# The first MLP product in 64x64 array tiles instead of 64x128

## The chip, the cores and the metric

The kernel runs on one core of a Trainium2 chip. The metric is the device time of one execution in microseconds, with all loads from and stores to the chip's memory. All arithmetic is in fp32.

## The reference

An RWKV-7 recurrence over 768 time steps, for 4 batches of 8 heads of 40 columns, followed by an MLP with an exact GELU over the 3,072 x 320 matrix that the heads make up:

```
for t in range(S):                       # S = 768, D = 40
    y[:, :, t] = einsum('bhd,bhde->bhe', rt, state)
    Sa = einsum('bhde,bhe->bhd', state, at)
    state = state * wt[:, :, None, :] - einsum('bhd,bhe->bhde', Sa, bt) \
            + einsum('bhd,bhe->bhde', vt, kt)
x = y.transpose(0, 2, 1, 3).reshape(B * S, H * D)     # 3072 x 320
h = x @ w_in                                          # 320 x 2048
g = 0.5 * h * (1 + erf(h / sqrt(2)))
out = g @ w_out                                       # 2048 x 320
```

## The kernel before

The 768 time steps are cut into 12 chunks of 64 (`c` is the chunk). In a chunk the recurrence is written as products: decays and their cumulative sums, the matrices `N` and `A`, the inverse of a triangular matrix (POOL builds it block by block, line 961 and line 963), the update of the state `st`, and `y`. Nearly all of these products are small: 64 or 40 rows by 64 columns of the TensorE array, with 64 or 104 columns streaming, or 32 by 32. They are issued through `mm` (line 193) in fours, so that each of the four 64x64 quarters of the array has one. In the timeline they are the groups of L193 with `64*64`, `40*64` or `32*32` (rows and columns of the array in use).

The result of a chunk, transposed, lies in `xt`: 5 slices of 64 of the 320 inputs, each with 256 columns (64 time steps of 4 batches). Both halves of the 128 partitions hold the inputs.

The MLP of a chunk is worked off between the attention steps of the following chunk. The step `mh(c, p)`, p from 0 to 7, is the first product. `w_in_sb` holds one half of the 2,048 hidden columns in each half of the partitions; a step takes 128 columns of each half, and for each of the 5 slices (`kt`) issues one matmul for each half `x`. Such a matmul uses 64 rows and all 128 columns of the array and streams 256 columns; the two halves' matmuls run at the same time, one in the upper and one in the lower 64 rows. The results accumulate over `kt` in PSUM, in one bank for each x; two steps (s = 0 and 1) fill the two halves of both banks. Then `ge(c, q)` applies GELU on ACT (line 1312) into `gt`, and frees the banks. The second product (line 1346, and line 1428 in the first chunks) uses 128 rows by 128 columns of the array. It is done by Strassen's scheme in seven products, with sums on DVE.

The order of all steps is written out by hand in `order(...)`, one list of tokens in which each token is one step. It sets the order of instructions on every engine at once: each step's instructions go to the engines' queues in the order of the list, and no engine changes it. The steps named in this text are in it as, for example, `mh.3.6 mh.3.7 ... ge.3.3`. PSUM is four pairs of banks, given out by `take` and given back by `drop`, in the same order.

Of the kernel before, what the change touches and what calls it, by code (L numbers as in the profile page):

```python
# [118 lines left out]
def kernel(  # L119
# [12 lines left out]
    nc = tc.nc  # L132
    B, H, S, D = r.shape
    DM, DF = moe_w_in.shape
    P = 128
    C = 64
    HP = 64
# [6 lines left out]
    NK = -(-DM // HP)  # L144
# [17 lines left out]
    def tile_of(name, shape, dtype=FP32):  # L162
        return const.tile(shape, dtype, name=name)
# [25 lines left out]
    def half(j, n=HP):  # L189
        return slice(j * HP, j * HP + n)  # L190
# [13 lines left out]
    xt = tile_of("xt", [P, NK, TB])  # L204
# [11 lines left out]
    w_in_sb = tile_of("w_in_sb", [P, NK, DF // 2])  # L216
# [1084 lines left out]
    @step  # L1301
    def mh(c, p):
        q, s = p // 2, p % 2
        ph = (bank if s else take)(f"ph{c}_{q}").rearrange("p x (s t) -> p x s t", s=2)
        for kt in range(NK):
            for x in range(2):
                nc.tensor.matmul(ph[:, x, s], w_in_sb[half(x), kt, p * P:(p + 1) * P], xt[half(x), kt],  # L1307
                                 start=kt == 0, stop=kt == NK - 1)

    @step  # L1310
    def ge(c, q):
# [155 lines left out]
```

## Time and profile before

| | us |
|---|---|
| three timed runs, median | 640.84 |
| lowest and highest | 638.62 and 642.05 |
| span of the profiled execution | 638.6 |
| TensorE busy in it | 621.4 |
| mean granted clock of TensorE | 0.995 of full |

The page gives no time for the profiled execution other than its span, from its first to its last instruction. In the rows below, an instruction group is written as line, engine, operation, written tile `<-` read tiles, then for TensorE rows`*`columns of the array in use, then partitions x elements of the operand, its type, and the count. PE is the matmul itself, PEld the load of the stationary operand. The profile shows each fp32 matmul as two records, and its weight load as two also. In a timeline row the first number is the start, the second the length from the first start to the last modelled end, in us; since matmuls overlap, a row can begin before the one ahead of it has ended.

### The profile page before, as it was taken

To read this page: it belongs to the slowest core of one execution; us is meant where nothing else is said; L and a number is where in the kernel's file an instruction comes from. 1 tells how busy PE (TensorE), PEld (TensorE's weight loads), DVE (VectorE), ACT (ScalarE), POOL (GpSimd) and SP (SyncE) were. 2 spreads that over 40 slices of the span, in tenths; PEclk is the share of its full clock that TensorE was granted. 3 is DMA by queue.
4 is the path that set the end of the run, shared out by engine and by line. 5 is a ranking of instruction groups with operands and counts; after the bars stand their busy time and mean duration, and the time that the engine had idled before them with its cause. 6 is when DMAs were issued, how large, how long until landed. Compare 5 with 4: busy or idle time off the path is not lost.

```text
span 638.6 us, 27896 instructions
## 1 busy us (share of the span) xinstructions
PE 621.4 (97%) x12418; PEld 548.3 (86%) x12418; DVE 457.9 (72%) x557; ACT 323.6 (51%) x456; POOL 380.3 (60%) x782
## 2 busy tenths in 40 slices
PE   7798999989999999999999999999999999999997
PEld 4576887778988988998998998998988998989987
DVE  0889889869887987875978877984883974753313
ACT  4468797874463465635544536563563365052021
POOL 4388289806845866848968548968805867910000
PEclk9799999999999999999999999999999999999999
DMA  9999488747478248395647445449346214210100
GB/s 136 181 162 178 91 178 187 143 104 137 91 135 149 59 98 159 64 147 111 110 84 133 76 93 107 88 88 157 68 92 109 41 37 84 42 26 3 36 7 21
DMA packets 246899, 64.07 MB, mean 100 GB/s; under 512 B 228380, under 2 KB 243644, under 8 KB 246780
## 3 DMA queue, kind: packets, MB, share of 16 engines
q1 hardware_dynamic: 246340, 62.01, 52.5%
q8 instruction: 97, 1.59, 1.1%
q10 hardware_dynamic: 440, 0.29, 0.2%
q14 instruction: 22, 0.18, 0.1%
HBM read 54.39 MB, written 3.93 MB: 91 GB/s over the span
## 4 chain that ended last, share of the span: by engine, by line
PE 76%; ACT 2%; DVE 0%; issue 0%; DVEq 0%
PE bank L1307 30%; PE bank L1346 27%; PE bank L193 19%; ACT Tt L937 0%; ACT SM L1154 0%; ACT L1312 0%; ACT spare L922 0%; DVE spare L864 0%; ACT st L1194 0%; ACT gt L1312 0%; ACT T L942 0%; DVE Tt L932 0%; ACT st L1192 0%; ACT Tt L1116 0%; DVE os L1299 0%
## 5 line engine op out<-in xcount | busy, mean ns | idle before, releaser
L1307 PE MATMUL bank<-xt,w_in_sb 64*128 64x256 f32 x1920 | 221.3, 381 | 0.2 <-ACT gt L1312 0.2
L961 POOL TENSOR_TENSOR tmp<-W,Nb 128x126 f32<-128x126 f32 (+22 forms) x341 | 164.4, 482 | 93.1 <-DVE Nb L927 67.6
L1307 PEld LDWEIGHTS bank<-xt,w_in_sb 64*128 64x128 f32 x1920 | 182.5, 187 | 25.1 <-issue 1.5
L963 POOL TENSOR_TENSOR W<-W,tmp 128x126 f32<-128x126 f32 (+22 forms) x341 | 168.8, 495 | 26.7
L1346 PE MATMUL bank<-w_out_sb,gt 128*128 128x160 f32 x704 | 101.1, 301 | 0.0
L1346 PEld LDWEIGHTS bank<-w_out_sb,gt 128*128 128x128 f32 x704 | 96.6, 190 | 2.2 <-issue 1.2
L1312 ACT ACTIVATE gt<-bank 128x1024 f32<-128x1024 f32 x48 | 48.7, 1024 | 94.9 <-PE bank L1307 94.6
L1175 DVE TENSOR_TENSOR SM<-bank,upper 128x832 f32<-128x832 f32 (+1 forms) x24 | 23.0, 988 | 20.3 <-PE bank L193 20.2
L1263 ACT COPY conv<-st 32x128 f32<-32x128 f32 (+2 forms) x55 | 28.0, 509 | 17.0 <-DVE st L1257 16.2
L1299 DVE TENSOR_TENSOR conv<-gt 128x1024 f32<-128x1024 f32 x11 | 14.2, 1290 | 25.1 <-ACT gt L1312 25.0
L1227 DVE TENSOR_TENSOR st<-bank,st 128x832 f32<-128x832 f32 (+1 forms) x22 | 21.2, 985 | 14.0 <-PE bank L193 14.0
L1346 PE MATMUL bank<-extra,conv 128*128 128x160 f32 x208 | 30.3, 300 | 0.0
L1299 DVE TENSOR_TENSOR os<-os,bank 128x160 f32<-128x160 f32 x44 | 13.8, 315 | 22.1 <-PE bank L1346 20.5
L1346 PEld LDWEIGHTS bank<-extra,conv 128*128 128x128 f32 x208 | 28.9, 190 | 0.1
L721 DVE TENSOR_TENSOR_SCAN kT<-spare,kT 128x256 f32<-128x256 f32 x36 | 26.6, 798 | 0.6 <-ACT kT L714 0.6
L1346 PE MATMUL bank<-extra,gt 128*128 128x160 f32 x176 | 25.8, 300 | 0.0
L1346 PEld LDWEIGHTS bank<-extra,gt 128*128 128x128 f32 x176 | 24.5, 190 | 0.1
L789 POOL TENSOR_TENSOR bk_rows<-bk_rows,part 128x640 f32<-128x640 f32 x9 | 14.3, 1591 | 14.3 <-ACT part L742 13.9
L1312 ACT ACT_TABLE_LOAD x17 | 21.8, 1283 | 0.3
L1346 PE MATMUL bank<-extra,SM 128*128 128x160 f32 x144 | 21.2, 300 | 0.0
L193 PEld LDWEIGHTS bank<-SM,Tt 64*64 64x64 f32 x768 | 17.1, 133 | 4.2 <-issue 2.3
L193 PE MATMUL bank<-SM,Tt 64*64 64x104 f32 (+1 forms) x768 | 19.3, 249 | 0.9 <-ACT Tt L1113 0.9
(220 smaller groups left out, 1101.1 us busy)
## 6 DMA issues: line engine op xcount, KB each, us to landing
bk_rows<-in_b_dram SPq DMA_DIRECT2D x24, 160.0 KB
bk_rows<-in_k_dram SPq DMA_DIRECT2D x24, 160.0 KB
out_dram<-os SPq DMA_DIRECT2D x46, 80.0 KB
VR<-in_v_dram SPq DMA_DIRECT2D x22, 160.0 KB
w_tile<-in_w_dram SPq DMA_DIRECT2D x36, 80.0 KB
a_pairs<-in_a_dram SPq DMA_DIRECT2D x18, 144.0 KB
a_pairs<-in_b_dram SPq DMA_DIRECT2D x18, 144.0 KB
v_pairs<-in_w_dram SPq DMA_DIRECT2D x18, 144.0 KB
```

The lines of the kernel that those rows point to most:

```text
L193: nc.tensor.matmul(o, lhsT, rhs, start=first, stop=True, skip_group_check=True)
L721: nc.vector.tensor_tensor_scan(logs[:, at:at + n], onward, logs[:, at:at + n], 0.0, ALU.mult, ALU.add)
L789: (nc.vector if q == "v" else nc.gpsimd).tensor_tensor(to, rows(k_of(c)), decays(c), ALU.mult)
L961: nc.gpsimd.tensor_tensor(t, W[:, BL // 2 - rows:, rest:rest + 1].to_broadcast([P, rows, rest]), Nb[:, rest:rest + 1, :rest].to_broadcast( ...
L963: nc.gpsimd.tensor_tensor(own, own, t, ALU.add)
L1175: nc.vector.tensor_tensor(SM[:, g, :, :, cols], pair_of(f"S{c}_", g).rearrange("p x i c -> p i x c")[:, :, :, cols], kept, ALU.mult)
L1227: nc.vector.tensor_tensor(to, pair_of(f"QY{c}_", g)[:, :, :, cols], to, ALU.add)
L1263: nc.scalar.copy(apart.rearrange("p e i g d -> p (e i g) d")[to_rows, :, to_col:to_col + n], st.rearrange("p e i g c -> p (e i g) c")[rows ...
L1299: nc.vector.tensor_tensor(to, one_, other, how)
L1307: nc.tensor.matmul(ph[:, x, s], w_in_sb[half(x), kt, p * P:(p + 1) * P], xt[half(x), kt], start=kt == 0, stop=kt == NK - 1)
L1312: nc.scalar.activation(gt[:, 4 * q:4 * q + 4].rearrange("p (x s) t -> p x s t", x=2), bank(f"ph{c}_{q}").rearrange("p x (s t) -> p x s t", ...
L1346: nc.tensor.matmul(po[:, n, :DM // 2], l_[:, f], r_[:, f], start=f == 0, stop=f == NF // 2 - 1)
```

## The change

In the step `mh` every matmul of 64 rows by 128 columns is split into two of 64 rows by 64 columns, one for each half of the 128 hidden columns. The four matmuls of one `kt` (two halves x of the rows, two halves of the columns) go to the four quarters of the array, in the order (upper rows, left columns), (lower, right), (upper, right), (lower, left). Each streams the same 256 columns as before, and each result lands where it did before: partitions 0 to 63 or 64 to 127 of the bank of x. A step has 20 matmuls instead of 10. The list in `order` and all other steps are unchanged.

```
         for kt in range(NK):
-            for x in range(2):
-                nc.tensor.matmul(ph[:, x, s], w_in_sb[half(x), kt, p * P:(p + 1) * P], xt[half(x), kt],
-                                 start=kt == 0, stop=kt == NK - 1)
+            for y in range(2):
+                for x in range(2):
+                    at = p * P + (x ^ y) * HP
+                    nc.tensor.matmul(ph[half(x ^ y), x, s], w_in_sb[half(x), kt, at:at + HP], xt[half(x), kt],
+                                     start=kt == 0, stop=kt == NK - 1, skip_group_check=True)
```

Here `P` is 128, `HP` is 64, `half(j)` the 64 partitions from 64 j on, and `ph` the pair of PSUM banks.

## The prediction

> **What bounds the kernel now.** I read the page first, then the timeline of TensorE alone, then its waits and the busy time by stage.
>
> ```profile
> span 638.6 us, 27896 instructions
> PE 621.4 (97%) x12418; PEld 548.3 (86%) x12418; DVE 457.9 (72%) x557; ACT 323.6 (51%) x456; POOL 380.3 (60%) x782
> PE 76%; ACT 2%; DVE 0%; issue 0%; DVEq 0%
> L1307 PE MATMUL bank<-xt,w_in_sb 64*128 64x256 f32 x1920 | 221.3, 381 | 0.2 <-ACT gt L1312 0.2
> ```
> ```profile
> 76.40:139.00 62.60, 59.61 (x1260) 48.05 (x1250) 52.53 (x73) 52.78 (x74) 44.53 (x77) 1.00 0.70 149
> 139.00:602.00 463.00, 462.25 (x9313) 420.59 (x9312) 343.55 (x387) 217.86 (x313) 293.77 (x590) 1.00 0.50 92
> ```
>
> TensorE is the bound: 97% busy, 76% of the chain that ended last. The stage table (length, then busy us of PE, PEld, DVE, ACT, POOL, then the granted clock) says it more sharply: from 139 to 602 us TensorE is idle for 0.75 us of 463, at the full granted clock. In that stage the next engine, DVE, has 343.55 us of work, 74%. The changed line, L1307, fills 221.3 us of the span, a third. So two questions decide: does TensorE need more or less time for L1307 and for what borders on it, and can the other engines follow.
>
> Busy time can't answer the first, because matmuls overlap. I read starts instead. The timeline of TensorE (start, length, then the group with its count):
>
> ```profile
> 291.07 4.59 PE L1307 MATMUL bank<-xt,w_in_sb 64*128 64x256 f32 x40
> 295.59 1.66 PE L193 MATMUL bank<-SM,Tt 64*64 64x104 f32 x64
> 297.18 2.43 PE L1307 MATMUL bank<-xt,w_in_sb 64*128 64x256 f32 x20
> 299.53 1.66 PE L193 MATMUL bank<-VR,bk_rows 64*64 64x104 f32 x64
> 301.01 1.61 PE L193 MATMUL bank<-SM,bk_rows 64*64 64x104 f32 x64
> 302.44 0.72 PE L193 MATMUL bank<-w_tile,cum_m 64*64 64x320 f32 x8
> 303.09 4.59 PE L1307 MATMUL bank<-xt,w_in_sb 64*128 64x256 f32 x40
> ```
>
> One step `mh` is 20 records: ten matmuls, and the profile shows each fp32 matmul as two records. Two tiles run at once, so 20 records are 10 waves of two. The bursts of 40 and of 20 differ by 4.59 - 2.43 = 2.16 us for 10 waves: **0.216 us a wave**, or 0.84 ns for each of its 256 columns. The whole step's streaming is 96 steps x 10 waves x 0.216 = 207 us of the 221.3.
>
> The rest is at the borders of the bursts. A burst of 20 begins at 297.18 and what follows begins at 299.53: 2.35 us, where 10 waves are 2.16, so 0.19 over. The burst of 40: 295.59 - 291.07 = 4.52, where 20 waves are 4.32: 0.20 over. I take 0.20 a burst. Half of it is the first wave:
>
> ```profile
> L1307 PE MATMUL bank<-xt,w_in_sb x1920: 376/376/480, 76.6 to 619.2; 64*128 64x256 f32 x192
> L1307 PEld LDWEIGHTS bank<-xt,w_in_sb x1920: 182/187/187, 76.6 to 619.0; 64*128 64x128 f32 x192
> L193 PEld LDWEIGHTS bank<-SM,Tt 64*64 64x64 f32 x768 | 17.1, 133 | 4.2 <-issue 2.3 <-POOL W L963 1.4 <-ACT conv L612 0.4
> ```
>
> The slowest matmul of L1307 takes 480 ns, the median 376: 0.10 us in which weights are loaded that in later waves load behind a running wave. The other 0.10 is paid on leaving.
>
> The attention bursts of 64 records (16 waves of four) show the same borders from their side. From 301.01 to 302.44, with 64-by-64 work before and after, is 1.43 us, or 0.0894 a wave. The one from 299.53 to 301.01, which comes out of L1307 and is followed by 64-by-64 work, takes 1.48: coming out of L1307 costs it 0.05. The one from 295.59 to 297.18 lies between two bursts of L1307 and takes 1.59: going into L1307 costs a further 0.11. So a border between 64x128 and 64x64 tiles is dear on both sides, and one between two kinds of 64x64 work costs nothing that these rows show. That it is the tile shape in the array and not the rows in use is seen here, where 64-row and 40-row work meet:
>
> ```profile
> 324.30 1.66 PE L193 MATMUL bank<-VR,late 64*64 64x104 f32 x64
> 325.78 1.11 PE L193 MATMUL bank<-rT,turned 40*64 40x64 f32 x64
> 326.82 4.59 PE L1307 MATMUL bank<-xt,w_in_sb 64*128 64x256 f32 x40
> ```
>
> 324.30 to 325.78 is 1.48 again: dear on entry from a 128-by-128 product, free on the way out to 40x64 work.
>
> **The change, part by part.** *The waves.* Each 64x128 matmul becomes two of 64x64, so a wave has four records in place of two, 960 waves as before, each still streaming 256 columns. The question is whether four tiles stream as fast as two. The four-tile rows say yes: 0.0894 us for 104 columns is 0.86 ns a column. The single-tile product is at 0.90:
>
> ```profile
> L1346 PE MATMUL bank<-w_out_sb,gt 128*128 128x160 f32 x704 | 101.1, 301 | 0.0
> 302.71 0.45 PE L193 MATMUL bank<-w_tile,cum_m 64*64 64x320 f32 x4
> ```
>
> That is 101.1 / 704 = 0.144 us for 160 columns. The longest four-tile wave, the second one of the 302.44 burst, starts at 302.71, so 0.27 us for 320 columns, 0.84 ns. Streaming does not depend on how many tiles share the array; this term is 0. Its bounds come from the same rows: at 0.86 ns a column a wave is 0.220 us, 960 x 0.004 = 4 us slower; at 0.83 (0.2125 a wave, rounding of the starts) 3 us faster. I take 0, from the row nearest in length, 320 columns.
>
> *Weight loads.* Two of 128 columns (187 ns) become four of 64 (133 ns). Inside a burst they hide behind the wave: in the 64x64 bursts four of them fit behind 0.0894 us, here they have 0.216. Without that cover a load would cost what it does at a first wave. Only the first wave after a border shows it: there 0.10 for 128 columns, 0.05 for 64.
>
> *The borders.* The timeline holds 48 bursts of L1307. Before 31 of them stands 64-column tile work, before 14 32-by-32 work, before 3 128-by-128 or other full-array work. After 36 stands 64-by-64 work, after 10 32-by-32, after 2 the second product. First and last of the 31 entries and of the 36 exits:
>
> ```profile
> 75.78 0.86 PE L193 MATMUL bank<-aT,nT 40*64 40x64 f32 x45
> 76.58 7.27 PE L1307 MATMUL bank<-xt,w_in_sb 64*128 64x256 f32 x60
> 83.77 0.41 PE L193 MATMUL bank<-VR,late 64*64 64x104 f32 x8
> ...
> 581.30 1.05 PE L193 MATMUL bank<-SM,Tt 64*64 64x64 f32 x60
> 582.29 2.43 PE L1307 MATMUL bank<-xt,w_in_sb 64*128 64x256 f32 x20
> 584.65 0.56 PE L193 MATMUL bank<-VR,bk_rows 64*64 64x64 f32 x22
> ```
>
> After the change L1307 has the same tile shape as that work, so those borders should go: an entry saves 0.11 + 0.10 = 0.21, an exit 0.10 + 0.05 = 0.15. The other 17 entries keep their border and save only 0.05 of first load; the other 12 exits save nothing. Sum: 31 x 0.21 + 36 x 0.15 + 17 x 0.05 = 6.5 + 5.4 + 0.85 = **12.8 us**.
>
> *What is late next.* The order on every engine is kept, and no DMA, wait or queue entry moves; each step after a burst simply starts earlier on TensorE. Whether its operands are there is seen in TensorE's waits; those from 76 to 139 us, then one row of those after:
>
> ```profile
> PE bank L193 <- ACT Js L1091: 1.5, 1, 1.5
> PE bank L193 <- ACT gt L1312: 1.4, 1, 1.4
> ...
> PE bank L1307 <- ACT gt L1312: 0.2, 1, 0.2
> ```
> ```profile
> 138.25 0.22 PE L193 MATMUL bank<-Tt,Js 32*32 32x32 f32 x2 [1.52 <-ACT Js L1091]
> ```
>
> The first ends at 138.25 us. At such a place TensorE already waits for another engine, and what it gains before is waited away, unless that engine too is served earlier. Four bursts lie before it, at three times about 0.36 and once 0.20: 1.3 us that I count as lost. After 139 us the view has no wait for another engine of over 0.2 us, and DVE at 74% has room, so I count the rest as kept: 12.8 - 1.3 = **11.5 us**.
>
> The profiled execution's span is 638.6; the timed runs go from 638.62 to 642.05 with the median 640.84, 2.2 above the span. I expect a span of about 627.1 and a median of 640.84 - 11.5 = **629.3**.
>
> *A rule of the skill that speaks against the change.* Against the 0.0894 us in which a wave of four records passes stands the Trainium skill, "TensorEngine Tiling (Array Packing)", Instruction Overhead: each matmul carries some 60 cycles of overhead on trn2. Were that charged for each of the 1,920 added records one after another, it would be an estimate from that page of 1,920 x 25 ns (60 cycles at the 2.4 GHz that the skill's page "TensorE: Matmul & The Clock Gate" gives) = 48 us, and the time would be about 677. This trace disagrees so far: at 25 ns a record four of them would need 0.100 us, more than the 0.0894 measured.
>
> **The rivals.** *Slower, two column tiles of one row half get in each other's way.* In the changed step tiles (row half x, columns 0 to 63) and (row half x, columns 64 to 127) stream the same 256 columns of `xt`, some ns apart. In the four-tile bursts above, the two tiles of a row half stream different columns; so no row shows this exact pattern. If they took turns, a wave would take 0.43 in place of 0.216: 960 x 0.216 = 207 us more, 836 in all. It decides from 0.012 us a wave (11.5 / 960), a wave of 0.228. Against it: four streams at once cost nothing in two row kinds.
>
> *Slower, the added records are not hidden.* The price from rows: 0.0894 / 4 = 0.0224 us a record, as an upper bound. 1,920 x 0.0224 = 43 us, so 629.3 + 43 = 672. It decides from 6 ns a record (11.5 / 1,920). Against it: a wave of four needs at most 0.0894 us for all its records and has 0.216. This is the mechanism of the skill's rule above.
>
> *Faster, but by about half.* The steps after a burst are attention steps that hang on DVE and ACT copies. If the 36 exits give their 0.15 back as new waits, 5.4 us go: 11.5 - 5.4 = 6.1, so 634.7. For it: 2.9 us of waits before 139 us show that such places exist. Against it: there is almost no wait later.
>
> *No change.* The border stays, because what is dear is not the tile shape but, say, the change of weights or of PSUM bank: then only the first loads shrink, 48 x 0.05 = 2.4 us, 638.4. Against it: the free borders at 301.01, 302.44 and 325.78, where weights and banks change too.
>
> **How the numbers follow.** About 0.5%, 3.2 us, is what a measurement of this kernel can tell from no change; the three runs spread over 3.4. Forecast, with its loss anywhere between nothing and a third: 0.66. Half of it: 0.16. No change: 0.08. Column tiles in each other's way: 0.06. Records not hidden: 0.04. So faster 0.82, same 0.08, slower 0.10. The low end: 12.8 kept in full plus the 3 us bound of the waves is 625.0; I stop at 625.5. The high end takes in the half case with the waves' upper bound partly paid: 636.5. What lies outside, the no-change case and the slower ones, has 0.18.
>
> **What would show it.** L1307 should be 64*64 64x256 with 3,840 records at a mean near 376 ns and weight loads at 133. A lone burst of one step between 64-by-64 work should last 2.16 us from its start to the next start, not 2.35, and a 64-record burst between two of them 1.43, not 1.59. TensorE's busy time should fall by about the time saved. A wave over 0.228 us, or new TensorE waits on ACT or DVE of over 0.15 us after most bursts, would make the prediction wrong.

## The result and the profile after

| | before | after |
|---|---|---|
| timed runs, median | 641.34 us of 4 | 649.3 us of 4 |
| lowest and highest | 638.62 and 642.05 | 645.87 and 650.47 |
| span of the profiled execution | 638.6 | 646.9 |

The ratio is 1.0123, with a 95% interval of 1.0087 to 1.0159: slower by 8 us, where 11.5 us of gain were forecast. The profiled execution after has a time of its own, 648.82 us, so 1.9 us lie around its span.

From the page of the kernel after (span, busy time, the DMA queue that carries instructions, the chain, the groups of the changed line):

```profile
span 646.9 us, 31736 instructions
PE 617.4 (95%) x14338; PEld 530.9 (82%) x14338; DVE 457.3 (71%) x557; ACT 323.9 (50%) x456; POOL 379.6 (59%) x782
q8 instruction: 112, 1.84, 1.3%
PE 74%; issue 2%; ACT 2%; DVE 1%; DVEq 0%; ACTq 0%
L1309 PE MATMUL bank<-xt,w_in_sb 64*64 64x256 f32 x3840 | 224.5, 379 | 6.7 <-issue 6.0
L1309 PEld LDWEIGHTS bank<-xt,w_in_sb 64*64 64x64 f32 x3840 | 161.3, 133 | 52.0 <-issue 11.1
```

The changed line runs as meant: 3,840 records of 64*64, mean 379 ns, loads of 133 ns. TensorE is busy for less time than before, 617.4 us against 621.4, and the span is still longer. So its idle time has grown: 638.6 - 621.4 = 17.2 us before, 646.9 - 617.4 = 29.5 us now, 12.3 more. In the chain the item issue has gone from 0 to 2%; it means that TensorE waited for nothing that the profile shows. The stage table (columns as in the prediction's) and TensorE's waits of the kernel after:

```profile
76.40:139.00 62.60, 60.14 (x1444) 46.76 (x1437) 53.20 (x74) 53.82 (x74) 44.93 (x77) 0.99 0.69 145
139.00:602.00 463.00, 449.95 (x10852) 399.75 (x10853) 341.80 (x385) 217.29 (x312) 292.52 (x590) 1.00 0.49 92
```
```profile
PE bank L193 <- issue: 10.1, 9, 2.2
PE bank L1309 <- issue: 6.0, 8, 1.2
PE bank L193 <- ACT Js L1091: 1.5, 1, 1.5
```

From 139 to 602 us TensorE now idles for 13.05 us, where it idled for 0.75. And the idle time has one name: issue, 16.1 us in 17 waits. Before there were three such waits and 2.5 us, a row of the waits of before that the prediction did not use:

```profile
PE bank L193 <- issue: 2.5, 3, 1.9
```

The timeline of TensorE after, the stretch that the prediction read in the kernel before:

```profile
283.99 2.77 PE L1309 MATMUL bank<-xt,w_in_sb 64*64 64x256 f32 x45
287.96 4.53 PE L1309 MATMUL bank<-xt,w_in_sb 64*64 64x256 f32 x75 [1.20 <-issue]
292.43 0.75 PE L193 MATMUL bank<-turned,spare 32*32 32x32 f32 x64
293.11 1.16 PE L193 MATMUL bank<-aT,kT 40*64 40x64 f32 x64
...
296.50 0.21 PE L193 MATMUL bank<-T,Js 32*32 32x32 f32 x2 [1.65 <-issue]
...
296.75 4.55 PE L1309 MATMUL bank<-xt,w_in_sb 64*64 64x256 f32 x80
301.11 1.61 PE L193 MATMUL bank<-SM,Tt 64*64 64x104 f32 x64
302.54 2.34 PE L1309 MATMUL bank<-xt,w_in_sb 64*64 64x256 f32 x40
304.70 1.61 PE L193 MATMUL bank<-VR,bk_rows 64*64 64x104 f32 x64
306.12 1.61 PE L193 MATMUL bank<-SM,bk_rows 64*64 64x104 f32 x64
```

Two things stand here. The forecast's borders are gone, to the digit: the lone step from 302.54 to 304.70 takes 2.16 us (2.35 before), the 64-record burst from 301.11 to 302.54 takes 1.43 (1.59 before). And two waits have come, one in the middle of a burst of the changed step, one in the middle of a group of 32-by-32 products, whose operands were all there. The saving at the borders is the forecast's too: from 301.11 to 306.12 are 5.01 us, where the same three bursts took 5.42 (295.59 to 301.01). That is 0.41 us, and the forecast was 0.21 for an entry, 0.15 for an exit and 0.05 for the exit of the burst ahead. Following the same matmuls through both traces, the places where the kernel after gains 0.1 us or more sum to some 12 us, and the places where it loses to some 19. Both sums shift by several us with which neighbouring shifts are taken as one place; only their difference is firm.

**Where the waits stand.** The queue that carries instructions has 112 packets in the page of after (above); the page of before has

```profile
q8 instruction: 97, 1.59, 1.1%
```

Both give 16.4 KB a packet. The change adds 1,920 matmul records and 1,920 records of weight loads to TensorE's stream, 3,840 instructions for 15 packets: **256 a packet**. And TensorE's 2 x 14,338 instructions of after make up 112 such blocks. A block is thus 128 matmul records with their loads. Counted in order, the waits of over 0.3 us in the kernel after begin at records 348, 985, 2257, 3148, 4295, 5443, 5698, 6463, 6719, 7994, 8632, 9015, 9907, 10291, 11184 and 12461. Their remainders by 128 fall evenly from 92 to 45, with no exception, because the stream also holds 116 instructions that wait for semaphores: counted with these, every wait stands at remainder 193 or 194 by 256. So each wait stands on the border of a block. In the rows above, 75 + 64 + 64 records and 53 of the 32-by-32 group lie between the two waits: 256 records, two blocks.

The packet records of the trace give the rest. For two waits of the kernel after (us: first record of the block, packet of the next block starts and lands, first record of the next block):

```
block begins   packet starts   packet lands   next block begins
   282.78         284.98          286.41           287.96
   292.89         293.95          295.15           296.50
```

My theory (A) from here: a block is fetched while the one ahead of it runs, and the fetch takes some 3.5 us or more from border to border. A block used up sooner leaves TensorE waiting for the rest. The second row's block held 1.97 us of work, and 1.97 + 1.65 of waiting is 3.62. The rivals: the four tiles disturb each other, or each added record costs time by itself, wherever it stands.

The firm part of A is the packet's landing. In all the kernels of this document, no block begins less than 1.19 us after its packet has landed, and every block that begins after a wait of over 0.3 us begins 1.20 to 1.87 us after it. The 3.6 us are only a rule of thumb, since packets do not start at a fixed time after a border. The first row's block held 3.98 us of work, more than 3.6, but the packet of the next one started only 2.20 us into it, and TensorE waited 1.20 us. Others start up to 3 us before the block ahead of theirs has begun to run. What sets their start was not tried.

### The profile page after: what moved, and what is told of

It is laid out like the page before. It is cut to its first block, busy times and chain, and to the rows that moved or that the text cites. A ratio compares the mean times of both kernels' runs of the same rounds, so it can differ in the third digit from the quotient of the medians.

```text
span 646.9 us, 31736 instructions
## 1 busy us (share of the span) xinstructions
PE 617.4 (95%) x14338; PEld 530.9 (82%) x14338; DVE 457.3 (71%) x557; ACT 323.9 (50%) x456; POOL 379.6 (59%) x782
## 4 chain that ended last, share of the span: by engine, by line
PE 74%; issue 2%; ACT 2%; DVE 1%; DVEq 0%; ACTq 0%
PE bank L1309 29%; PE bank L1348 26%; PE bank L193 18%; DVE kT L721 0%; ACT L1314 0%; ACT L734 0%; ACT spare L922 0%; ACT T L942 0%; ACT Tt L937 0%; DVE spare L864 0%; ACT wpT L734 0%; ACT st L1194 0%; ACT kT L738 0%; ACT gt L1314 0%; DVE Tt L932 0%
## 5 line engine op out<-in xcount | busy, mean ns | idle before, releaser
L1309 PE MATMUL bank<-xt,w_in_sb 64*64 64x256 f32 x3840 | 224.5, 379 | 6.7 <-issue 6.0
L1309 PEld LDWEIGHTS bank<-xt,w_in_sb 64*64 64x64 f32 x3840 | 161.3, 133 | 52.0 <-issue 11.1
L1299 DVE TENSOR_TENSOR conv<-gt 128x1024 f32<-128x1024 f32 x11 | 14.1, 1280 | 24.3 <-ACT gt L1314 24.2
L1299 DVE TENSOR_TENSOR os<-os,bank 128x160 f32<-128x160 f32 x44 | 13.8, 314 | 21.8 <-PE bank L1348 20.1
L193 PE MATMUL bank<-SM,Tt 64*64 64x104 f32 (+1 forms) x768 | 20.6, 248 | 1.8 <-issue 1.5
L193 PEld LDWEIGHTS bank<-SM,Tt 64*64 64x64 f32 x768 | 19.0, 133 | 3.7 <-issue 2.3
```

The source lines that it names most:

```text
L193: nc.tensor.matmul(o, lhsT, rhs, start=first, stop=True, skip_group_check=True)
L1299: nc.vector.tensor_tensor(to, one_, other, how)
L1309: nc.tensor.matmul(ph[half(x ^ y), x, s], w_in_sb[half(x), kt, at:at + HP], xt[half(x), kt], start=kt == 0, stop=kt == NK - 1, skip_group_ ...
```

## The experiments

**The old tiles with the new number of records.** Each matmul keeps its 64x128 tile and is split into two of 128 streaming columns.

```
-            for x in range(2):
-                nc.tensor.matmul(ph[:, x, s], w_in_sb[half(x), kt, p * P:(p + 1) * P], xt[half(x), kt], ...)
+            for u in range(2):
+                for x in range(2):
+                    nc.tensor.matmul(ph[:, x, s, u * P:(u + 1) * P], w_in_sb[half(x), kt, p * P:(p + 1) * P],
+                                     xt[half(x), kt, u * P:(u + 1) * P], ...)
```

> The step mh keeps its 64x128 tiles, two at once, but each matmul is split in two of 128 streaming columns, so it has 40 matmul records and 40 weight loads as in the changed kernel. Theory A (instruction supply: TensorE's instructions arrive in blocks of 256 and a block that is used up in less than about 3.5 us makes the engine wait for the next): no border is saved, the waits on issue appear as in the changed kernel, 10 to 22 us more than before, 651 to 663 us. Theory B (the four 64x64 tiles disturb each other, or the tile shape itself makes the waits): the tile shape is the old one, so only 960 x 2.3 ns = 2 us for the doubled number of waves, 643 us, and no new waits on issue.

Measured: 660.85 us against 640.12, ratio 1.0324 (1.0266 to 1.0381), within the range of A. Its waits:

```profile
PE bank L193 <- issue: 8.8, 8, 2.3
PE bank L1308 <- issue: 3.3, 7, 0.9
```

The waits come without any new tile, so disturbed tiles can't be their cause; a price for each added record they don't yet exclude. This kernel is 20.7 us above its runs of before, the kernel after 8.0 above its own. The difference, 12.8 us (20.73 - 7.96), is close to what the prediction had worked out for the borders, but it is not their price. From its start to the next group's, a burst of two steps takes 4.665 us here and one of one step 2.432, so a step's streaming takes 2.233 us where it took 2.16: some 7 us over the 96 steps. The expectation had put the doubled waves at 2 us. The waits on issue are 4.1 us fewer than in the kernel after (12.1 against 16.1), and three stretches of 3.4 us after 139 us are at half clock, where the kernel after has one, from 137.3 us.

**The new tiles with the old number of records.** The loop over y runs once, so half of the first product is left out, and a wave has two 64x64 records.

```
-            for y in range(2):
+            for y in range(1):
```

> The step mh uses 64x64 tiles but only two of the four (upper rows with left columns, lower rows with right columns), so half of the first product is left out; records stay at 20 per step and each wave still streams 256 columns. Theory A: the borders go and no waits on issue come, 641.3 - 12.8 = 628.5 us, 625 to 631. Theory B with the tile shape as the cause: the waits on issue stay, 640 us or more. (B with four tiles as the cause agrees with A here.)

Measured: 632.63 us against 640.12, ratio 0.9875 (0.9835 to 0.9916). That is 1.6 us above the range of A. In the trace the gains sum to some 12 to 13 us, again by which shifts are taken together. Two issue waits are left: 1.93 us at the start, where before has 1.92, and 0.64 us at one later border. Other waits take back some 5 us; the largest:

```profile
PE bank L751 <- DMA r_pairs<-in_r_dram: 1.5, 1, 1.5
```

So the tile shape saves about what was forecast, and 7.5 us of it reach the end when no block is added.

**The kernel before, moved by half a block.** 32 tiny products (32x32) are added in the warm-up step, four instructions each: 128 instructions. All the rest is as before, but the block borders fall elsewhere in it.

```
+        for n in range(32):
+            mm(pt[:BL, 0, :BL], w_in_sb[:BL, 0, :BL], w_in_sb[:BL, 0, :BL])
```

> The kernel before, with 32 tiny 32x32 matmuls (64 matmul records and 64 weight loads, 128 instructions) added at the start, at about 25 us where TensorE waits for loads. Theory A: the same work, but each border of an instruction block falls 128 instructions earlier in the work; the order before has its borders where a block lasts long, and half a block on they fall in the attention bursts: 5 to 15 us slower, 646 to 656, with waits on issue. Theory B and any theory of engines or tiles: under 1 us, 641 to 642.

Measured: 664.89 us against 640.12, ratio 1.038 (1.0332 to 1.0429). That is 24.8 us more, and 9 us above the range of A. The products themselves, run at half clock at the start, take 2.0 of it (the warm-up takes 4.79 us in before and 6.80 here). Waits, then the timeline where the prediction's first rows lay:

```profile
PE bank L193 <- issue: 14.1, 11, 2.1
```
```profile
296.28 0.75 PE L193 MATMUL bank<-turned,spare 32*32 32x32 f32 x64
296.96 1.16 PE L193 MATMUL bank<-aT,kT 40*64 40x64 f32 x64
...
300.00 0.21 PE L193 MATMUL bank<-Tt,Js 32*32 32x32 f32 x2 [1.32 <-issue]
```

The short attention products now fill one block by themselves: 1.97 us of work, and then a wait. In the kernel before a border cut this stretch so that each part shared its block with slow records. The waits of theory A come here with no tile and no step changed; the loss is larger than the waits, and the last section sets the clock beside it.

**By a whole block, and the kernel after by half a block.** `range(64)` in before, `range(32)` in after.

> The kernel before with 64 tiny matmuls at the start instead of 32: 256 added instructions, one whole block, so the borders of the blocks fall where they fell before. Theory A: the loss of the 128-instruction shift is gone although twice as much was added, 640 to 643 us. If the added matmuls themselves (their time, their place in PSUM) had made that loss: 660 us or more.

> The changed kernel with the same 128 added instructions at the start. Theory A: its borders move too, so its waits on issue stand at other places and its time changes by several us, 650 to 660; it was not at its worst before. If the order of the borders were of no account for it: 649.3 us within 1.

Measured: before moved by 256, 645.42 us against 640.58 (1.0078; 1.005 to 1.0107); after moved by 128, 657.27 (1.0265; 1.0219 to 1.0312). A whole block brings the borders back to their places, and 20 of the 25 us go: it is the place that counts, not how much was added. The first is still 2.4 us above the range of A, 640 to 643, and the second within its own; most of the 4.8 us that remain in the first are the 64 products. From the timelines of before and of before moved by 256:

```profile
27.69 4.86 PE L193 MATMUL bank<-w_in_sb 128*128 128x512 f32 x6
32.48 2.08 PE L193 MATMUL bank<-turned,st 64*64 64x64 f32 x64
```
```profile
27.67 8.69 PE L193 MATMUL bank<-w_in_sb 128*128 128x512 f32 x134
36.29 1.91 PE L193 MATMUL bank<-turned,st 64*64 64x64 f32 x58
```

The warm-up takes 4.79 us there and 8.62 here, 3.8 more; 1.2 us more of issue waits (3.7 against 2.5) make 5.0. Moved by the same 128 instructions, the kernel after is faster than before, 657.27 against 664.89; but their borders do not fall on the same work.

**By small steps.** The block count can be made ahead. I took the starts of before without their issue waits, moved the borders, and summed 3.6 us less the work of each block that had less: 3.8 us unmoved, 1.6 at 24 instructions, 11.4 at 64, 19.0 at 128. Two more runs, `range(6)` and `range(16)`:

> The kernel before with 6 more tiny products at the start, 24 TensorE instructions, so that every block border of 256 instructions falls 24 instructions earlier in the work. Counted on the trace of before: with a block that takes less than 3.6 us stalled up to 3.6 us, the sum of stalls is 3.8 us at shift 0 (2.5 measured), 1.6 us at shift 24, 11.4 at shift 64, 19.0 at shift 128 (11.6 more than before were measured there) and 3.8 again at shift 256. Theory A, the place of the borders decides: stalls of 1 to 2 us, and a median of 637.5 to 641. Rival, any product added at the start delays the rest, by the 4.8 us that 64 of them cost, 0.075 us each: 641.6. Rival, the code is at its best place only where it was drawn up and any shift that isn't a whole block costs about what 128 did: 655 or more.

> The kernel before with 16 more tiny products at the start, 64 TensorE instructions, a quarter of a block. Theory A: by the count on the trace of before the stalls are 11.4 us against 19.0 at shift 128; scaled by what was measured there (14.1 of 19.0) some 8.5 us of waits put down to issue, 6 more than before, and with the half-clock windows that follow such waits (24.8 us of time for 11.6 us of waits at shift 128) a median of 648 to 656: between that of 0 and that of 128. Rival, products added at the start delay the rest by 0.075 us each: 642.3.

Measured: moved by 24, 641.83 us against 640.05 (1.0021; 0.9999 to 1.0042); moved by 64, 655.02 (1.0212; 1.0185 to 1.0239). The second lies in its range; its waits:

```profile
PE bank L193 <- issue: 6.5, 5, 2.5
PE bank L1309 <- issue: 3.8, 5, 1.4
```

That is 10.3 us, where the count gave 11.4 and the expectation 8.5. The first is a miss: 0.8 us above the range of A and next to the rival's 641.6. Its waits on issue are 3.1 us in all, above the 1 to 2 forecast and above the 2.5 unmoved, so the count does not resolve differences this small. Nor do the products simply delay the rest: its trace is 0.03 us behind that of before at 60 us and 1.2 us ahead at 130 us. It loses that again by 143 us, where its clock is at half for 3.4 us from 136.8 us, as that of before is not.

**Blocks used up as fast as they can be.** Two steps of nothing but 64x64x64 products are added, one at 49 us and one at the end.

```
+    def dense(i, n):
+        pt = take(f"dense{i}").rearrange("p x (s t) -> p x s t", t=C)
+        for m in range(n):
+            for j in range(2):
+                for e in range(2):
+                    mm(pt[half(e ^ j), j, m % 8], ident[half(j), half(j)], ident[half(j), half(j)])
```

> The kernel before, with two bursts of 64x64 matmuls of 64 columns that wait for nothing and whose results nobody reads: 512 matmuls (2,048 instructions, 8 blocks) at about 38 us, while the DMA queues are at 0.9, and 640 matmuls (2,560 instructions, 10 blocks) at the very end, when no load is left. In short bursts such work passes 8 instructions in 0.058 us, 1.9 us a block. Theory A: both bursts settle at 3.3 to 3.7 us a block, about 34 us for the last; if the DMA load sets the price, the first is well above the last. Theory B: 1.9 us a block in both, 19 us for the last.

One run, 702.59 us. The timeline of TensorE, and the stage table of these two stretches:

```profile
54.25 2.09 PE L193 MATMUL bank<-ident 64*64 64x64 f32 x128 [2.57 <-issue]
57.98 2.09 PE L193 MATMUL bank<-ident 64*64 64x64 f32 x128 [1.64 <-issue]
61.44 2.09 PE L193 MATMUL bank<-ident 64*64 64x64 f32 x128 [1.36 <-issue]
```
```profile
54.25:68.34 14.09, 8.37 (x512) 7.82 (x512) 0.00 (x0) 0.00 (x0) 5.32 (x18) 1.00 0.02 5
671.97:690.15 18.18, 10.46 (x640) 9.77 (x641) 0.00 (x0) 0.00 (x0) 0.00 (x0) 1.00 0.02 5
```

Exactly 128 records, then a wait, again and again. The starts lie 3.73 and 3.46 us apart, the work is 2.09. DMA is busy for 2% of the stretches (the column before the last), so this is not a crowded queue but a round trip. The first burst came at 49 us and not at 38, where the queues would have been full; so whether their load raises the price is not answered by it. With the packets:

```
block begins   packet starts   packet lands   next block begins
    54.25          55.42          56.62            57.98
    57.98          59.13          60.08            61.44
    61.44          62.47          63.45            64.89
   671.97         673.09         674.42           675.72
```

1.0 to 1.2 us after the border the packet starts, 0.95 to 1.3 us it takes, and 1.3 to 1.45 us later the first instruction runs. In these blocks the next fetch begins only after the border; the sum is 3.45 to 3.75 us for 256 instructions, 13.5 to 14.6 ns each (one block of each burst took 4.0). The Trainium skill, "Runtime: NRT & Kernel Launch", Instruction fetch mechanics, says that the stream is refilled in blocks of 16 KiB, 256 instructions, one being fetched while the current one runs; these runs agree. It adds that the cost of a border is mostly hidden; here that holds mostly for blocks with more than about 3.6 us of work, and not always (table below).

**Can both be had?** A kernel whose first product goes to quarters only where no block becomes too short. Four such kernels were run: a list of 31 of the 96 steps; two lists of 44 and 45 with small products added to move the borders; 27 late steps with 40 small products in one attention step.

```
+            if f"{c}.{p}" in in_quarters:
+                ...                         # the loop of after
+                continue
```

> 31 of the 96 steps mh (16 of the 48 bursts) use the 64x64 tiles, the others stay at 64x128. The bursts were picked by counting instructions along the trace of before, so that as few blocks of 256 as possible are used up in less than 3.6 us. They save 12 entries at 0.21, 13 exits at 0.15 and 4 first loads at 0.05 us: 4.7 us. Theory A: 640.1 - 4.7 = 635.4 us, with no more waits on issue than before, 633 to 638, faster than both kernels. A theory in which each step in 64x64 tiles costs its share of the loss, wherever it stands: 640.1 + 8.0 x 31 / 96 = 642.7 us.

> 44 of the 96 steps mh in 64x64 tiles, picked again by counting instructions, none of them ahead of 143 us, where loads and ACT set the pace anyway. Eight bursts are led in by 16 to 96 instructions of tiny matmuls (256 in all, their results are written over), which move the borders of the blocks out of the attention bursts. The borders of the bursts save 5.4 us, the fillers cost about 1.8. Theory A: 640.6 - 3.6 = 637.0 us if no wait on issue is added, 634 to 639. If each converted step cost its share: 640.6 + 8.0 x 44 / 96 = 644 us.

> 45 of the 96 steps in 64x64 tiles, another choice (none ahead of 195 us), with fillers of 240 instructions before six bursts. The borders save 7.0 us, the fillers cost 1.7. Theory A: 640.6 - 5.3 = 635.3 us if no wait on issue is added, 632 to 639; this choice leaves less room at the borders of the blocks than the other one, so its spread is wider. If each converted step cost its share: 644 us.

> The 27 late steps of the first picked set (none ahead of 184 us) in 64x64 tiles, and instead of its early ones 40 tiny 32x32 matmuls (160 instructions, as many as the early steps had added) at about 137 us, where TensorE waits 1.5 us for an ACT copy; so the blocks' borders in the later steps fall as in the first picked set. The borders save 3.6 us, the fillers lie in the wait. Theory A: 641 - 3.6 = 637.4 us, 635 to 640. If a converted step cost its share: 641 + 8.0 x 27 / 96 = 643 us.

| | us | before | ratio (95%) |
|---|---|---|---|
| 31 steps | 638.68 | 640.58 | 0.9971 (0.9947 to 0.9995) |
| 44 steps, filled | 649.0 | 641.25 | 1.0134 (1.0099 to 1.0169) |
| 45 steps, filled | 640.86 | 641.25 | 0.999 (0.9966 to 1.0014) |
| 27 late steps | 639.99 | 641.2 | 0.9986 (0.996 to 1.0012) |

Theory A had put them at 635.3 to 637.4 us; only the fourth came within its range, 635 to 640. Only the first is under both kernels beyond its interval, by 0.3%, which is little for the best of four. From 150 us to the end its trace gains 2.9 us on that of before; ahead of that it loses 3.4, among others to transfers that TensorE now reaches too early:

```profile
PE bank L751 <- DMA r_pairs<-in_r_dram: 2.4, 1, 2.4
PE bank L1319 <- DMA xt<-xt: 1.4, 2, 1.0
```

The 44-step version lost most visibly at its fillers, of which it has most in the first step of chunk 1; timeline, and the stage from 134 to 150 us:

```profile
138.70 5.33 PE L193 MATMUL bank<-xt,w_in_sb 64*128 64x32 f32 x48
```
```profile
134.00:150.00 16.00, 14.51 (x376) 13.21 (x369) 5.32 (x6) 7.46 (x13) 0.00 (x0) 0.68 0.59 117
```

The expectation had 1.8 us for all 256 instructions of the fillers, so some 0.7 for these 48 records and their loads; they took 5.33. The clock is at half for 10.2 us from 137.1 us on, so it fell ahead of them, and its mean is 0.68 in this stage. A load of 128 columns takes 330 ns there, and a record streams only 32 columns; that no running wave hides such loads is my reading and was not tried. The two others can't be told from before. Their waits on issue are 4.7 and 4.4 us, where before has 2.5, so part of the saving went there.

## Why the prediction was wrong

The block count, by kernel. The work of a block is the time between its borders less the issue wait. Short is a block with under 3.6 us of work.

| kernel | blocks | short | short with a wait behind | issue waits, us | of them behind longer blocks |
|---|---|---|---|---|---|
| before | 96 | 4 | 0 | 2.5 | 2.5 |
| after | 111 | 28 | 12 | 16.1 | 5.6 |
| more records, same tiles | 111 | 21 | 7 | 12.1 | 5.7 |
| new tiles, old count | 96 | 5 | 1 | 2.6 | 1.9 |
| before, moved by 128 | 97 | 15 | 8 | 14.1 | 3.1 |
| before, moved by 256 | 97 | 4 | 0 | 3.7 | 3.7 |
| after, moved by 128 | 112 | 26 | 15 | 20.2 | 5.5 |
| before, moved by 24 | 96 | 6 | 3 | 3.1 | 2.2 |
| before, moved by 64 | 96 | 18 | 9 | 10.3 | 2.5 |

All these waits stand on borders of blocks. The last column holds in each kernel one of 1.4 to 2.5 us at about 25 us, which before has too. More than half of the short blocks have no wait behind them: the next packet had landed early enough. So the number of short blocks tells where waits are to be feared, not their sum.

*What held.* The waves: the step of 302.54 takes the 2.16 us of 10 waves of 0.216; so the term 0 and its place between the bounds were right, and the rival of column tiles in each other's way is refuted. The borders: 12.8 us forecast, some 12 in the trace of after and 12 to 13 in that of half the product; around the step of 302.54 the 0.41 us are met to the digit. TensorE's busy time fell, as said it would, though by 4.0 us and not 11.5.

*The step that failed is "What is late next".* It asked only whether operands are there, from ACT, DVE and DMA, and held that no queue entry moves. It did not ask whether the instructions are there, though the change adds 3,840 of them to TensorE's own queue. Before, the changed step used four instructions in 0.216 us, so a block of 256 lasted 13.8 us; after, eight, and a block lasts 6.9 us. That is more than 3.6, so the changed step alone should not run dry. But a burst of 64 attention records takes 1.43 us for half a block, 2.9 us for a block, and a block of 32-by-32 and 40-by-64 products holds 1.97. What had kept such blocks long was the slow records beside them, and there are now twice as many of those for the same time. So 4 short blocks became 28, and 2.52 us of waits on issue became 16.15: 10.5 us behind short blocks, the rest behind blocks of up to 5.0 us whose next packet started late. The 13.6 us that came are more than all that the borders saved.

*The rival of unhidden records had the right sign, not the mechanism.* It put a price on each added record, 0.0224 us, and the chance of 0.04 rested on the wave having room for four. The room inside a wave is real. The limit lies over 256 instructions, across the bursts, where no wave shows it. Moving the kernel before by half a block, which adds 64 records and 2.0 us of work, costs 24.8 us, and after by as much some 9 (1.0265 against 1.0123): a price per record explains neither.

*The net.* 13.6 us more of issue waits and a half-clock window of up to 1.7 us, less some 12 us of borders, is some 3 us of the span's 8.3. The other 5 us are small delays that I can't put on one cause.

## What to carry to other kernels

A change that splits instructions for the sake of the array also draws more of the instruction stream: count instructions over windows as long as a block, not only inside a wave, and look for stretches of short instructions whose block was kept long by slow neighbours. An issue row in the waits of an engine that should be fully fed is the sign, and the proof is that such waits lie whole blocks of instructions apart and end when the packet of the next block has landed. Since the borders' place alone moved this kernel by over 20 us, a few per cent between two versions with different instruction counts say little on the edit itself until one of them has also been run with its borders moved.

## What the runs showed of the hardware that was not expected

*Half-clock windows of 3.4 us follow waits as short as 1.2 us.* The clock of before moved by 128 falls to 0.5 in five windows of 3.4 us and one of 6.8 after 139 us; one begins at 246.4 us, after the wait of 1.40 us that ends at 245.4. Stage rows of that kernel, around two of them:

```profile
134.00:152.00 18.00, 16.09 (x448) 13.16 (x450) 12.02 (x13) 13.28 (x19) 1.46 (x6) 0.91 0.55 113
240.00:256.00 16.00, 14.60 (x388) 12.16 (x388) 9.99 (x10) 9.03 (x13) 6.61 (x19) 0.89 0.52 98
```

23.9 us at half clock cost up to 12 us, which with 11.6 us more of issue waits and the 2.0 us of products comes to 25.6, near the 24.8 that were measured. The Trainium skill, "TensorE: Matmul & The Clock Gate", Part 1, gives windows of 3,413 ns and the half rate after a whole idle one; the length agrees, but here a window at half clock followed 3.4 us in which TensorE had been idle for only 1.15 to 2.05 us, six times in this kernel. In the kernel after, waits of 1.65 and 1.67 us at 296.5 and 490.3 us had none behind them. What decides was not tried.
